# More deferred products per routing hop, gathered rows turned by TensorE, and a new order for the last dense experts

## The chip, the cores and the metric

The kernel runs on one core of a Trainium2 chip. The metric is the device time of one execution in microseconds (us). Three runs of the kernel before gave 862.59, 863.86 and 866.21 us; their median, 863.86 us, is the time that the change is compared with. A separate execution was taken with the profiler.

## The reference

Three layers follow one another on 1536 tokens of 512 numbers. Attention has 8 heads of 64, with a local window of 96 keys and 8 global keys. The first mixture computes all 4 experts for every token and adds them with given shares. The second mixture sends each token to one of 8 experts, 192 tokens to each, in the order of all gate logits:

```python
attn = softmax(q @ k.T * scale + bias) @ v            # per head, masked
x = attn.transpose(0, 2, 1, 3).reshape(1536, 512)
p = domain_probs / (domain_probs.sum(-1, keepdims=True) + 1e-09)
for e in range(4):
    out += p[:, e:e + 1] * (np.maximum(x @ w1[e], 0.0) @ w2[e])
logits = out @ w_gate
for idx in np.argsort(-logits.flatten()):             # 12288 pairs (token, expert)
    tok, e = idx // 8, idx % 8
    if assigned[tok] < 0 and counts[e] < 192:
        assigned[tok] = e; counts[e] += 1
y[mask_e] = np.maximum(out[mask_e] @ v1[e], 0.0) @ v2[e]
```

## The kernel before

Tokens lie in 12 blocks of 128. Numbers are split in two float16 parts, high and low, and a product is made of three matmuls (high by high, high by low, low by high). Weights arrive as float32, 1 MB at a time, and are prepared in steps: ScalarE squares a half (L469, tile `junk`) to find a power of two, TensorE sums over the partitions (L473, tile `pw`), VectorE makes the scale (L330, L334, L335), ScalarE writes the high part (L580, tile `w`) and VectorE the low part (L494, tile `w`). One call of `pump` issues one such step and first starts any load that has a free buffer (`w_load`, L413). Squares of a half are issued only when `wait` pumps have passed since its load was issued (`WAITS`).

The order on each engine is the order in which the program issues; the engines work through it in turn, and so does the DMA queue that SyncE (SP) issues.

**The stage of the last dense experts** (`phase3`, 354 to 571 us of the span) computes the first layers of experts 2 and 3, forms the gate logits of each block and ranks the pairs. Its order is written out by hand in the table `ORDER3`: `a` are products on TensorE, `r`, `h` and `l` the ReLU and its two halves (L862 or L860, L584/L582/L580, L1584; a letter behind a slash gives the engine, A ScalarE, V VectorE, G GpSimd), `mturn` and `turn` transposes of the second-layer weights by DMA (L932, tiles `wth`, `wtl`), `mprod` and `prod` the small products that use them (L940), `start` the end of the preparation of expert 3's weights, `row` a transposed block for the logits (L956), `lm`, `lo`, `rr`, `cm`, `rc`, `ct`, `rk` the logits and the ranking (`ct` on TensorE, L1039; `cm` on VectorE, L1019 to L1024; `rk` writes tile `R`, L1049). `fill` issues a twelfth of a deferred product: the second layers of experts 3 and 2 for one block take 24 matmuls of 512 columns (L1072), two to a fill, 288 fills in all. When a block is done VectorE adds it to `y` (L1086).

**The route** (`route`, 579 to 631 us) finds the cut of each expert in 7 rounds. A round has four hops from VectorE to TensorE and back, and at each hop `between` issues some fills, by the list `HOPS`, and one `pump`. A round counts on TensorE (L1206), reads the count (L1209), spreads it (L1215), and does so twice.

**The tail** (631 to 684 us) issues the remaining fills, three at a time with a pump, and beside them the side work of finished blocks: `add`, a square (L1092), a scale, the two halves of the rows (L1115 to L1120, tile `xs`), and their store to memory (L1123, tensor `rows`).

**The routed experts** (684 us to the end) gather 2 x 96 rows for each expert with an indirect DMA from GpSimd (L1274, tile `g`), turn them so that columns lie on partitions (`gather_T`, a DMA transpose on SP, L1283, tile `xg`) and compute `m_g1` (L1305) and `m_g2` (L1325), with a pump for every step or so. An expert has 96 matmuls of 192 columns in each of its two layers; in the first, every 24 end in one ReLU on ScalarE, `H` (L860).

Of the kernel before, what the change touches and what calls it, by code (L numbers as in the profile page):

```python
# [6 lines left out]
F32 = mybir.dt.float32  # L7
# [125 lines left out]
    mturn3 mprod1 a21 mturn4 xh0/V h0/G pump.7 l0/G pump.8 pump.9 a30 mturn5 a31 xl0 r2/V h1/V a40 row0 l1/G r3/A
    pump.10 pump.11 pump.12 pump.13 h2/G pump.14 mprod2 norm1 a41 pump.15 a50 pump.16 mturn6 a51 pump.17 sc1 mturn7
    l2/G mprod3 xh1/V a60 a61 mgate start h3/A turn0 l3/G turn1 prod0 turn2 r4/A turn3 turn4 a70 a71 xl1 r5/A h4/A
    h5/V turn5 prod1 l4/V row1 prod2 turn6 a00.1 a01.1 r6/V l5/V norm0.1 r7/V h6/G h7/A turn7 sc0.1 sp prod3 l6/G
    r0.1/A l7/G a10.1 gate lm fill a11.1 lo rr xh0.1/G r1.1/V cm1 cm0 rc0 rc1 lm.1 cm2 ct0 ct1 fill.1 rc2 ct2 cm4 cm3
    rc3 rc4 h0.1/G cm5 a20.1 ct3 a21.1 lo.1 cm6 rr.1 ct4 h1.1/V rc5 rc6 cm7 xl0.1 fill.2 ct5 rc7 l0.1/V l1.1/V r2.1/V
    ct6 a30.1 ct7 cm0.1 a31.1 cm1.1 rc0.1 rk a40.1 cm2.1 ct0.1 rc1.1 ct1.1 h2.1/G a41.1 r3.1/A a50.1 rc2.1 cm3.1
    h3.1/A ct2.1 rc3.1 row0.1 ct3.1 cm4.1 l2.1/V a51.1 rc4.1 norm1.1 cm5.1 cm6.1 sc1.1 ct4.1 a60.1 l3.1/V a61.1  # L140
    xh1.1/A a70.1 r4.1/V a71.1 h4.1/A r5.1/V xl1.1 l4.1/V rc5.1 row1.1 a00.2 fill.3 rc6.1 h5.1/G norm0.2 ct5.1 r6.1/V
    l5.1/G a01.2 sp.1 h6.1/G a10.2 r7.1/V fill.4 l6.1/V sc0.2 h7.1/G l7.1/V lm.2 a11.2 xh0.2/A lo.2 ct6.1 rr.2 r0.2/V
    xl0.2 r1.2/A cm0.2 lm.3 fill.5 rc0.2 cm7.1 ct0.2 rc7.1 cm1.2 fill.6 ct7.1 h1.2/G row0.2 cm2.2 fill.7 cm3.2 norm1.2
    a20.2 rk.1 rc1.2 lo.3 rc2.2 ct1.2 ct2.2 fill.8 fill.9 cm5.2 cm4.2 a21.2 rc3.2 sc1.2 rc4.2 ct3.2 h0.2/G rc5.2 a30.2
    l0.2/V cm6.2 ct4.2 r2.2/A ct5.2 l1.2/V rc6.2 fill.10 cm7.2 rr.3 ct6.2 a31.2 cm0.3 cm1.3 r3.2/V rc7.2 rc0.3 ct7.2
    a40.2 h3.2/A xh1.2/V rk.2 h2.2/A rc1.3 xl1.2 cm2.3 ct0.3 row1.2 a41.2 l3.2/G a50.2 rc2.3 a51.2 ct1.3 cm3.3 a60.2
# [15 lines left out]
    h0.5/A ct5.7 cm6.7 l0.5/V a21.5 rc6.7 a30.5 h1.5/V ct6.7 r2.5/A h2.5/A rc7.7 a31.5 rr.8 xl0.5 fill.24 lo.9 l1.5/V
    ct7.7 a40.5 cm0.8 rc0.8 cm1.8 rc1.8 cm2.8 row0.5 rk.7 rc2.8 r3.5/A a41.5 ct0.8 ct1.8 cm4.8 cm3.8 rc4.8 ct2.8 cm5.8
    h3.5/A fill.25 rr.9 a50.5 ct3.8 fill.26 rc5.8 ct4.8 a51.5 ct5.8 cm6.8 a60.5 cm0.9 a61.5 rc6.8 ct6.8 l2.5/G rc0.9
    cm7.8 cm1.9 fill.27 r4.5/A ct7.8 cm2.9 l3.5/G r5.5/A norm1.5 a70.5 rc1.9 rk.8 a71.5 fill.28 fill.29 sc1.5 h4.5/A
# [1716 lines left out]
```

## Time and profile before

| what | value |
|---|---|
| median of three runs | 863.86 us (862.59 to 866.21) |
| the profiled execution's own time | 861.97 us |
| its span | 860.2 us |
| TensorE busy (matmul) | 777.3 us, 90% of the span |
| VectorE busy | 608.4 us, 71% |
| ScalarE busy | 502.2 us, 58% |
| GpSimd busy | 206.4 us, 24% |
| mean granted clock of TensorE | 0.962 of full speed |

Full speed is 2.4 GHz and the other level is 1.2 GHz, 0.5 of it. A busy share is a mean over stages with different limits, so the table only says where to look: TensorE is nearly full, and what it lacks lies in a few stretches. 1.8 us of the execution lie outside the span.

### The profile page before, as it was taken

What the parts mean: (1) busy time and instruction counts of PE and PEld (TensorE: products, weight loads), DVE (VectorE), ACT (ScalarE), POOL (GpSimd) and SP (SyncE); (2) the same over time, 40 slices, a digit from 0 to 9 for tenths busy, and PEclk for the clock granted to TensorE, in tenths of its full rate; (3) what the DMA queues carried; (4) which work ended last, traced back from release to release, by engine and by line L of the source; (5) the groups of instructions that cost most, each with busy time, mean ns of one, the idle gap of its engine ahead of it and who ended that gap; (6) DMA issues with size and microseconds to landing.
All of it is one profiled execution on the core that took longest, in us unless ns stands there. A gap on an engine that the chain in (4) does not pass through costs nothing. (4 is left out here: it accounts for less than half of the span.)

```text
span 860.2 us, 21736 instructions
## 1 busy us (share of the span) xinstructions
PE 777.3 (90%) x8916; PEld 600.1 (70%) x8920; DVE 608.4 (71%) x1467; ACT 502.2 (58%) x1004; POOL 206.4 (24%) x238
## 2 busy tenths in 40 slices
PE   3688999999999999999999999979998757999996
PEld 3477767777777767678888887534443357888996
DVE  5998888777763644547879999986674625797890
ACT  5887786745352323334557979631056417989852
POOL 3553352332442224240210112000000022222221
PEclk9689999999999999999999999989999869999999
DMA  8996769664447311691333320249014279899811
GB/s 272 265 191 140 130 154 171 120 136 88 99 73 207 104 51 51 125 178 31 75 71 69 77 59 26 63 103 330 34 32 140 76 237 332 253 265 335 174 38 38
DMA packets 219652, 116.38 MB, mean 135 GB/s; under 512 B 187424, under 2 KB 187424, under 8 KB 219552
## 3 DMA queue, kind: packets, MB, share of 16 engines
q1 hardware_dynamic: 217504, 108.64, 50.6%
q0 software_dynamic: 2048, 6.34, 3.1%
q8 instruction: 70, 1.15, 0.6%
q14 instruction: 30, 0.25, 0.1%
HBM read 69.30 MB, written 12.63 MB: 95 GB/s over the span
## 5 line engine op out<-in xcount | busy, mean ns | idle before, releaser
L886 PEld LDWEIGHTS <-w 128*128 128x128 f16 x3456 | 248.1, 98 | 37.9 <-issue 4.1
L886 PE MATMUL pH<-xT,w 128*128 128x128 f16 (+1 forms) x3168 | 252.9, 235 | 2.2 <-ACT H L860 1.6
L1072 PE MATMUL pY<-w,xT 128*128 128x512 f16 x384 | 120.7, 386 | 4.6 <-DVE y L1086 4.6
L897 PE MATMUL pY<-w,hh 128*128 128x512 f16 x384 | 114.7, 381 | 0.0
L1033 ACT ACTIVATE Cj<-C 128x256 bf16<-128x256 bf16 (+11 forms) x88 | 75.3, 855 | 28.2 <-DVE C L1024 21.6
L1305 PEld LDWEIGHTS <-w 128*128 128x128 f16 x768 | 66.4, 101 | 28.5 <-DMA xg<-g 16.2
L1072 PE MATMUL pY<-w,hl 128*128 128x512 f16 x192 | 74.1, 386 | 0.0
L897 PE MATMUL pY<-w,hl 128*128 128x512 f16 x192 | 73.1, 381 | 0.0
L860 ACT ACTIVATE H<-pH 128x512 f32<-128x512 f32 (+1 forms) x70 | 38.4, 554 | 55.1 <-PE pH L886 34.4
L1305 PE MATMUL pH<-xg,w 128*128 128x192 f16 x528 | 51.5, 259 | 19.5 <-DMA xg<-g 17.0
L1072 PEld LDWEIGHTS <-xT 128*128 128x128 f16 x384 | 36.5, 99 | 42.1 <-issue 8.6
L1325 PE MATMUL pR<-hh,w 128*128 128x192 f16 x512 | 64.9, 246 | 0.0
L1325 PEld LDWEIGHTS <-w 128*128 128x128 f16 x768 | 63.3, 98 | 2.0 <-issue 1.9
L1325 PE MATMUL pR<-hl,w 128*128 128x192 f16 x256 | 63.0, 246 | 0.0
L1022 DVE TENSOR_SCALAR C<-w,Lg 128x1024 bf16<-128x1024 f32 (+7 forms) x98 | 58.8, 615 | 0.6 <-PE pw L1039 0.4
L762 ACT ACTIVATE t<-pS,mx,ec 128x256 f32<-128x256 f32 (+1 forms) x96 | 51.6, 541 | 2.2
L777 POOL TENSOR_TENSOR pp<-t,pp 128x512 f16<-128x512 f32 (+1 forms) x34 | 40.1, 1183 | 44.4 <-ACT pp L580 35.9
L494 DVE SCALAR_TENSOR_TENSOR w<-w,wsr,w 128x1024 f16<-128x1024 f32 x32 | 40.4, 1279 | 10.0 <-ACT w L580 9.9
L584 DVE TENSOR_SCALAR hh<-H 128x384 f16<-128x384 f32 (+1 forms) x53 | 20.9, 396 | 37.5 <-ACT H L860 37.0
L897 PEld LDWEIGHTS <-hh 128*128 128x128 f16 x384 | 32.9, 98 | 19.6
L1452 POOL TENSOR_TENSOR hl<-H,hh 128x512 f16<-128x512 f32 x26 | 32.9, 1265 | 56.3 <-DVE hh L584 31.7
L469 ACT ACTIVATE junk<-w 128x2048 f16<-128x2048 f32 x16 | 30.5, 1906 | 25.4 <-DMA w<-in_moe_w_dram 25.4
(298 smaller groups left out, 1537.7 us busy)
## 6 DMA issues: line engine op xcount, KB each, us to landing
w<-in_moe_w_dram SPq DMA_DIRECT2D x16, 1024.0 KB, 13.0
raw<-in_moe_w_dram SPq DMA_DIRECT2D x16, 1024.0 KB, 7.8
hl<-in_moe_w_dram SPq DMA_DIRECT2D x8, 1024.0 KB, 5.5
y<-in_moe_w_dram SPq DMA_DIRECT2D x4, 1024.0 KB, 6.7
xT<-in_moe_w_dram SPq DMA_DIRECT2D x4, 1024.0 KB, 11.5
rows<-xs SPq DMA_DIRECT2D x12, 260.0 KB, 2.1
x<-in_k_dram SPq DMA_DIRECT2D x12, 256.0 KB, 3.3
x<-in_q_dram SPq DMA_DIRECT2D x12, 256.0 KB, 3.9
```

The lines of the kernel that those rows point to most:

```text
L494: V.scalar_tensor_tensor(l, r[:, d2], sc, h, op0=OP.mult, op1=OP.subtract)
L762: s.nc.scalar.activation(t[:, hh], ps[:, hh], AF.Exp, bias=mx[:, 1, hh:hh + 1], scale=e[:, 0:1], accum_out=s.SU[j][:, 2 * g + hh:2 * g + h ...
L777: (G if eng == "G" else V).tensor_sub(pl[:, x], t, ph[:, x])
L860: s.nc.scalar.activation(H, ps, AF.Relu, scale=HS)
L886: nc.tensor.matmul(o[f], w[:, d, 128 * (f0 + f):128 * (f0 + f) + 128], x[:, :, c], start=(d == 0 and i == 0), stop=(d == 3 and i == 2))
L897: nc.tensor.matmul(py, l[:, f], w[:, f], start=(f == 0 and i == 0), stop=(f == 7 and i == 2))
L1022: V.tensor_scalar(C[:, 8 * i:8 * i + n], x[:, :n, e], l, None, op0=OP.is_ge)
L1033: s.nc.scalar.activation(x, C, AF.Copy, accum_out=s.AC[j][:, 1, e:e + 1])
L1072: nc.tensor.matmul(py, a[:, f], w[:, f], start=(n == 0), stop=(n == 23))
L1305: nc.tensor.matmul(ps[0][:, f % 2], w[:, d, 128 * f:128 * f + 128], xg[:, :, c], start=(k == 0), stop=(k == 11))
L1325: nc.tensor.matmul(ps[0][:, d % 2], w[:, f, 128 * d:128 * d + 128], h[:, f], start=(k == 0), stop=(k == 23))
L1452: (nc.gpsimd if eng == "G" else nc.vector).tensor_sub(x[1], P.pop((e, j, c)), x[0])
```

## The change

Four things change. The order of `phase3` is another one (the same 775 entries; two lines of the table are shown). The hops of rounds 2 to 7 issue 8, 2, 5 and 1 fills where they issued 8, 1, 4 and 1. In the tail the pumps stop when 18 or fewer fills are left, and none goes with the side work; `WAITS[1]`, the wait before squares in the stage of the routed experts, goes from 13 to 18. And the gathered rows of experts 0 and 1 are turned by 32 matmuls against the identity, which ScalarE and VectorE copy out of PSUM, four copies each; experts 2 to 7 keep the DMA transpose.

```diff
-    norm0 sc0 a00 pump pump.1 mturn0 a01 pump.2 mturn1 a10 pump.3 pump.4 pump.5 pump.6 r0/A mprod0 a11 r1/V a20 mturn2
+    pump a00 mturn0 pump.1 pump.2 pump.3 pump.4 mturn1 norm0 pump.5 a01 a10 mturn2 r0/A mturn3 pump.6 sc0 xh0/A xl0
...
-HOPS = [0, 1, 4, 1, 8, 1, 4, 1, 8, 1, 4, 1, 8, 1, 4, 1, 8, 1, 4, 1, 8, 1, 4, 1, 8, 1, 4, 1, 4, 7]
-WAITS = [4, 13, 6, 2]
+HOPS = [0, 1, 4, 1] + [8, 2, 5, 1] * 6 + [4, 7]
+LASTFILLS, PUMPR = 18, 1
+WAITS = [4, 18, 6, 2]
...
+    def gather_turn(s, e):
+        nc, g = s.nc, s.GX[e]
+        xg = s.ex.tile([128, 2, 8, 96], F16, name="xg")
+        for u in range(2):
+            for a in range(2):
+                ps = s.pH.tile([128, 4, 96], F32, name="pH")
+                for i in range(4):
+                    nc.tensor.matmul(ps[:, i], g[:, u, 512 * a + 128 * i:512 * a + 128 * i + 128], s.identh[:96, :96],
+                                     start=True, stop=True)
+                o = xg[:, u, 4 * a:4 * a + 4]
+                if a:
+                    nc.vector.tensor_copy(o, ps)
+                else:
+                    nc.scalar.activation(o, ps, AF.Copy)
+        s.GX[e], s.GG[e] = xg, g
...
             while fills:
                 fill(3)
-                s.pump(1)
+                if len(fills) > LASTFILLS:
+                    s.pump(PUMPR)
             while s.side:
                 s.side_step()
-                s.pump(1)
...
-            s.gather_T(0)
-            s.gather_T(1)
+            s.gather_turn(0)
+            s.gather_turn(1)
             s.rawfree += [raw2] * 4 + two(s.wc, 1)
             s.loadlimit = len(s.jobs)
             s.pump(WAITS[3])
```

In the table the engines of some entries change too. Over the stage VectorE has 14 `r` where it had 18, 10 `h` where it had 7, and 27 `l` where it had 29; for the first pair of blocks GpSimd has 3 `l` where it had 6. `start` comes after the ten products to `a41`; it came after the fourteen to `a61`.

The order on SP around the gathers, before: stores of rows, the four transposes of gathered rows, then eight loads of weights of 1 MB (`raw`, `w_11172`, `w_10031`).

```order
L413 DMA w_10031<-in_moe_w_dram 128x4x512
L1123 DMA rows<-xs 128x1040 x3
L413 DMA w_10031<-in_moe_w_dram 128x4x512
L1123 DMA rows<-xs 128x1040 x9
L1283 DMA_TRANSPOSE xg<-g 128x8x96 x4
L413 DMA raw<-in_moe_w_dram 128x4x512 x5
L413 DMA w_11172<-in_moe_w_dram 128x4x512 x2
L413 DMA w_10031<-in_moe_w_dram 128x4x512
L1283 DMA_TRANSPOSE xg<-g 128x8x96 x2
```

The same place now (the changed file's lines are one higher here):

```order
L1124 DMA rows<-xs 128x1040 x3
L414 DMA w_10031<-in_moe_w_dram 128x4x512 x2
L1124 DMA rows<-xs 128x1040 x9
L414 DMA raw<-in_moe_w_dram 128x4x512 x5
L414 DMA w_11216<-in_moe_w_dram 128x4x512 x2
L414 DMA w_10031<-in_moe_w_dram 128x4x512
L1284 DMA_TRANSPOSE xg<-g 128x8x96 x2
```

The eight loads no longer stand behind transposes that wait for the gathers, and the first three stores of rows stand ahead of both loads of the tail.

ScalarE at the start of the routed experts, before: high parts of expert 1's first layer, a square, the ReLUs of expert 0 and 1.

```order
L580 ACTIVATE w_11153<-raw,wsr 128x2x512 x2
L580 ACTIVATE w_11153<-w_10031,wsr 128x2x512 x2
L469 ACTIVATE junk,wss<-raw 128x2048
L860 ACTIVATE H<-pH 128x384 x2
L860 ACTIVATE H<-pq 128x384
L580 ACTIVATE w_11287<-w_10031,wsr 128x1024
L860 ACTIVATE H<-pH 128x384
L580 ACTIVATE w_11287<-w_10031,wsr 128x1024
L860 ACTIVATE H<-pH 128x384
L469 ACTIVATE junk,wss<-raw 128x2048 x2
L860 ACTIVATE H<-pq 128x384
```

And now, with the copies of the turned rows (`xg`) in it:

```order
L581 ACTIVATE w_11153<-raw,wsr 128x2x512 x2
L581 ACTIVATE w_11153<-w_10031,wsr 128x2x512
L1301 ACTIVATE xg<-pH 128x384 x4
L581 ACTIVATE w_11153<-w_10031,wsr 128x2x512
L470 ACTIVATE junk,wss<-raw 128x2048
L861 ACTIVATE H<-pH 128x384 x2
L861 ACTIVATE H<-pq 128x384
L581 ACTIVATE w_11331<-w_10031,wsr 128x1024
L861 ACTIVATE H<-pH 128x384
L581 ACTIVATE w_11331<-w_10031,wsr 128x1024
L861 ACTIVATE H<-pH 128x384
L581 ACTIVATE w_11331<-raw,wsr 128x1024
```

The copies stand ahead of one high part and of the first square, and the two squares that stood behind the fifth ReLU come later.

## Rows read from the trace of the kernel before

**Rows 1.** Busy time by stretch: us, PE, PEld, DVE, ACT, POOL (instructions), clock, DMA, GB/s.
```profile
354.40:390.00 35.60, 32.96 (x415) 28.96 (x414) 18.72 (x47) 10.13 (x16) 10.87 (x10) 0.95 0.95 157
480.00:553.00 73.00, 71.98 (x972) 57.80 (x969) 70.28 (x201) 58.84 (x108) 13.16 (x17) 1.00 0.22 56
553.00:571.00 18.00, 13.11 (x144) 6.97 (x143) 17.69 (x50) 12.61 (x17) 0.24 (x3) 0.81 0.36 89
631.00:684.00 53.00, 45.65 (x224) 20.23 (x221) 30.55 (x61) 30.79 (x58) 0.98 (x9) 0.97 0.27 91
698.00:730.00 32.00, 25.86 (x260) 24.89 (x261) 14.23 (x35) 19.05 (x25) 4.86 (x4) 0.87 1.04 328
730.00:800.00 70.00, 64.55 (x769) 62.77 (x767) 56.32 (x96) 67.36 (x86) 18.72 (x22) 1.00 1.02 285
```

**Rows 2.** Timeline at the turned weights of expert 3, ScalarE and TensorE.
```profile
367.62 0.60 ACT L860 ACTIVATE H<-pH 128x512 f32<-128x512 f32 x1 [6.17 <-POOL hl L1584]
...
380.82 0.18 PE L940 MATMUL pq<-wg,wtl 128*128 128x8 f16 x1 [1.92 <-DMA wtl<-w]
```

**Rows 3.** Who TensorE waited for, 320 to 580 us: total, times, longest.
```profile
PE pw L1039 <- DVE R L1049: 4.2, 2, 3.1
PE pq L940 <- DMA wtl<-w: 2.6, 2, 1.9
```

**Rows 4.** VectorE's groups, 354 to 571 us: count, busy us, mean ns, idle before; one `h`.
```profile
L1584 DVE TENSOR_TENSOR hl<-H,hh 128x512 f16<-128x512 f32 x15 | 11.1, 748 | 0.2 <-ACT hh L580 0.2
L862 DVE TENSOR_SCALAR H<-pH 128x512 f32<-128x512 f32 x12 | 8.1, 684 | 2.4 <-PE pH L886 2.3
...
394.69 0.42 DVE L584 TENSOR_SCALAR hh<-H 128x512 f16<-128x512 f32 x1
```

**Rows 5.** One round of the route: busy time, two rows of TensorE, one of VectorE.
```profile
602.91:610.47 7.56, 7.56 (x55) 3.36 (x55) 4.47 (x18) 0.00 (x0) 0.00 (x0) 1.00 0.19 69
...
607.07 0.59 PE L1072 MATMUL pY<-w,xT 128*128 128x512 f16 x2
607.72 0.59 PE L1072 MATMUL pY<-w,xT 128*128 128x512 f16 x2
...
610.47 0.19 DVE L1209 TENSOR_SCALAR_CACHE_REDUCE vt<-pq 8x40 f32<-8x40 f32 x1 [1.19 <-PE pq L1206]
```

**Rows 6.** Timeline of the tail: a square on ScalarE, and the last low part on VectorE.
```profile
657.03 1.91 ACT L469 ACTIVATE junk<-w 128x2048 f16<-128x2048 f32 x1 [2.96 <-DMA w<-in_moe_w_dram]
...
664.83 0.59 PE L1072 MATMUL pY<-w,xT 128*128 128x512 f16 x2 [2.00 <-DVE y L1086]
...
666.66 1.28 DVE L494 SCALAR_TENSOR_TENSOR w<-w,wsr,w 128x1024 f16<-128x1024 f32 x1 [1.45 <-ACT w L580]
```

**Rows 7.** Chain that ended last, from the last rows to the first routed product.
```profile
685.89 2.02 DMA rows<-xs
...
693.19 3.96 DMA g<-rows,idx
```

**Rows 8.** Issues of gathers at 693, 718 and 758 us, and transposes at 693: median us to landing.
```profile
xg<-g SPq DMA_TRANSPOSE x2, 3.5
g<-rows,idx POOLq DMA_INDIRECT x1, 4.0
...
g<-rows,idx POOLq DMA_INDIRECT x1, 6.6
...
g<-rows,idx POOLq DMA_INDIRECT x2, 11.3
```

**Rows 9.** Timeline between the tail and the routed experts: VectorE, TensorE, SP.
```profile
685.77 2.48 DVE L494 SCALAR_TENSOR_TENSOR w<-raw,wsr,w 128x1024 f16<-128x1024 f32 x2
...
697.92 6.63 PE L1305 MATMUL pH<-xg,w 128*128 128x192 f16 x48 [15.71 <-DMA xg<-g]
698.48 4.64 SPq L413 DMA_DIRECT2D raw<-in_moe_w_dram  x5
```

**Rows 10.** ScalarE and TensorE at the start of the routed experts: timeline, then a wait.
```profile
704.05 1.91 ACT L469 ACTIVATE junk<-raw 128x2048 f16<-128x2048 f32 x1 [15.20 <-DMA raw<-in_moe_w_dram]
...
724.78 0.47 ACT L860 ACTIVATE H<-pH 128x384 f32<-128x384 f32 x1
...
PE pw L473 <- ACT junk L469: 6.5, 6, 1.9
```

**Rows 11.** Turning by TensorE earlier in the kernel: ns min/median/max, first and last start.
```profile
L664 PE MATMUL pH<-identh,xs x8: 219/258/315, 46.9 to 48.0; 128*128 128x128 f16 x8
```

More of the change, by code (lines that the diff above doesn't have):

```diff
@@ L131 @@
 ORDER3 = """
-    norm0 sc0 a00 pump pump.1 mturn0 a01 pump.2 mturn1 a10 pump.3 pump.4 pump.5 pump.6 r0/A mprod0 a11 r1/V a20 mturn2
[L133 to L146, printed above, removed]
@@ L162 @@
[L162 to L165, printed above, removed]
-    ct0.9 ct1.9 l4.5/G h5.5/A fill.30 cm4.9 fill.31 rc2.9 fill.32 r6.5/A fill.33 l5.5/V cm3.9 h6.5/A fill.34 r7.5/A
@@ new lines @@
+    pump.7 mprod0 a11 mturn4 a20 h0/V l0/G r1/V pump.8 a21 pump.9 h1/A mprod1 mturn5 a30 pump.10 mturn6 pump.11 l1/G
+    mturn7 row0 pump.12 mprod2 a31 pump.13 r2/V mprod3 norm1 pump.14 a40 h2/V mgate a41 pump.15 pump.16 pump.17 r3/V
+    start l2/V r4/A a50 h3/A a51 turn0 sc1 a60 turn1 turn2 xh1/V prod0 a61 turn3 xl1 l3/G prod1 a70 a71 r5/A turn4
+    turn5 h5/G h4/A prod2 l4/V a00.1 row1 l5/V turn6 turn7 norm0.1 r6/A h6/G prod3 a01.1 r7/A h7/G gate a10.1 l7/V
+    l6/V lm sc0.1 lo a11.1 xh0.1/A r0.1/V rr a20.1 cm0 cm2 cm1 rc0 ct0 rc1 ct1 sp rc2 cm3 ct2 rc3 lm.1 ct3 xl0.1 fill
@@ new lines @@
+    cm6 cm5 fill.1 h0.1/V fill.2 r1.1/A fill.3 cm4 rc4 rc5 h1.1/A ct4 l0.1/G lo.1 rc6 row0.1 a21.1 ct5 ct6 cm7 l1.1/G
+    rc7 rr.1 cm0.1 r2.1/A cm1.1 a30.1 ct7 rc0.1 rc1.1 fill.4 a31.1 rk norm1.1 ct0.1 r3.1/V h2.1/A a40.1 cm2.1 ct1.1
+    rc2.1 a41.1 l2.1/V sc1.1 cm3.1 rc3.1 ct2.1 cm4.1 cm5.1 xh1.1/V rc4.1 rc5.1 h3.1/G xl1.1 a50.1 ct3.1 ct4.1 r4.1/V
+    cm6.1 a51.1 l3.1/V a60.1 r5.1/V a61.1 row1.1 a70.1 a71.1 norm0.2 a00.2 rc6.1 h4.1/A l4.1/V r6.1/A h5.1/G sc0.2
+    ct5.1 l5.1/G ct6.1 a01.2 cm7.1 r7.1/A h7.1/A a10.2 h6.1/G l6.1/V r0.2/A l7.1/G fill.5 xh0.2/A lm.2 lo.2 a11.2
@@ new lines @@
+    xl0.2 r1.2/V rr.2 cm0.2 sp.1 rc0.2 lm.3 fill.6 rc7.1 ct0.2 lo.3 ct7.1 cm1.2 h0.2/A cm3.2 fill.7 a20.2 rc1.2 cm2.2
+    row0.2 a21.2 rc2.2 rk.1 rc3.2 ct1.2 h1.2/A rr.3 ct2.2 ct3.2 cm5.2 l0.2/V fill.8 fill.9 cm4.2 cm6.2 rc4.2 r2.2/A
+    rc5.2 a30.2 ct4.2 rc6.2 ct5.2 l1.2/G ct6.2 h2.2/V cm7.2 a31.2 cm0.3 rc7.2 a40.2 r3.2/A cm1.3 rc0.3 ct7.2 a41.2
+    rk.2 ct0.3 a50.2 rc1.3 h3.2/V ct1.3 cm2.3 a51.2 norm1.2 rc2.3 cm3.3 ct2.3 rc3.3 ct3.3 fill.10 sc1.2 cm5.3 a60.2
+    l2.2/V xh1.2/V l3.2/G cm6.3 cm4.3 rc4.3 a61.2 xl1.2 a70.2 r4.2/A r5.2/V rc5.3 a71.2 h5.2/A row1.2 ct4.3 h4.2/V
@@ new lines @@
+    fill.39 rc5.9 lo.10 cm6.9 rr.10 ct5.9 lm.11 fill.40 fill.41 cm0.10 fill.42 fill.43 rc0.10 lo.11 rc6.9 rr.11 ct0.10
+    ct6.9 cm3.10 fill.44 cm1.10 fill.45 cm7.9 fill.46 fill.47 rc1.10 fill.48 fill.49 fill.50 ct1.10 ct7.9 fill.51
+    fill.52 fill.53 cm2.10 fill.54 rc2.10 ct2.10 fill.55 cm4.10 fill.56 rk.9 fill.57 rc4.10 fill.58 fill.59 ct3.10
+    fill.60 cm5.10 cm6.10 fill.61 fill.62 ct4.10 fill.63 rc5.10 ct5.10 rc6.10 fill.64 fill.65 fill.66 cm0.11 fill.67
+    fill.68 rc0.11 fill.69 fill.70 cm7.10 ct6.10 fill.71 cm1.11 fill.72 ct7.10 ct0.11 fill.73 rc1.11 cm2.11 rk.10
@@ L176 @@
+    ct1.11 rc2.11 cm3.11 ct2.11 cm4.11 cm5.11 ct3.11 cm6.11 rc4.11 rc5.11 fill.74 rc6.11 fill.75 fill.76 fill.77
+    ct4.11 fill.78 fill.79 fill.80 ct5.11 fill.81 fill.82 fill.83 fill.84 sp.5 ct6.11 fill.85 fill.86 fill.87 cm7.11
+    fill.88 ct7.11 fill.89 fill.90 fill.91 fill.92 fill.93 fill.94 rk.11 fill.95
 """.split()
```

44 lines of the change are left out of this document (20 added, 24 removed).

## The prediction

> **What bounds the kernel now.** I read the busy time by stretch first, then who TensorE waited for, then the timelines of the places that the change touches.
>
> In the stage of the last dense experts TensorE works 32.96 of the first 35.6 us, at a mean clock of 0.95, and VectorE only 18.72 [rows 1]. From 480 us on VectorE is full too: 70.28 of 73 us, then 17.69 of 18 while TensorE falls to 13.11 [rows 1]. What ends the stage is VectorE's ranking; TensorE waits 4.2 us for it there [rows 3].
>
> In the route a round takes 7.56 us, and TensorE is busy in all of them [rows 5]. In the tail TensorE idles 53 - 45.65 = 7.35 us with no other engine full [rows 1]. The stalls start on ScalarE: a square waits 2.96 us for its weights, VectorE's low part waits for the high part behind it, and TensorE stands 2.00 us because the sum of a finished block (L1086) comes late and its PSUM buffer with it [rows 6].
>
> Between the last rows and the first routed product everything is idle but the chain: rows to memory, gathers, transposes [rows 7, 9]. From 698 to 730 us TensorE works 25.86 of 32 us, at 0.87 of its clock; from 730 to 800 us ScalarE is full, 67.36 of 70 [rows 1]. So the routed experts run at ScalarE's pace, and how early it gets its work decides.
>
> A difference under 0.5%, 4.3 us, is about what a measurement of this kernel cannot tell from none.
>
> **The order of the last dense experts.** The same work is issued in another order, so nothing is removed on TensorE. What can be won is idle time: 35.6 - 32.96 = 2.64 us at the start, with 5% of clock there, some 1.8 us [rows 1], and 3.0 us of VectorE's own idle time from 480 us on (2.72 + 0.31) [rows 1]. That is 7.4 us, the lower end of the time. VectorE's work gets 4 `r` less at 0.684, 3 `h` more at 0.42 and 2 `l` less at 0.75 us: -2.74 + 1.26 - 1.50 = -3.0 us [rows 4]. The other end: the eight transposes for `mprod` now come in a row and `mprod2` and `mprod3` two products earlier or more; two waits like the longest of before, 1.92 us [rows 2], would cost 4 us where about 2.6 are lost now, so some 2 us worse allowing for the clock.
>
> I take -3 us, for one reason that rows carry. ScalarE stood 6.17 us at 367.6 us behind a GpSimd `l` [rows 2]; the last high parts of expert 3's weights were queued behind that, then their transposes, and at their end TensorE stood 1.92 us [rows 2]. Now GpSimd has half of those `l`, and `start` is issued four products earlier, so these transposes begin about that ReLU's wait, half of it or more, sooner. The 1.92 us and most of the clock's 1.8 go, less what arises anew. The end of the stage keeps its order (the last counts wait for VectorE as before), so I expect no more from there than VectorE's 3.0 us of work would allow, and count none of it. What is late next is row 11's comparisons on VectorE.
>
> **The hops.** Twelve fills move out of the tail into six rounds. A fill is two matmuls; three start in 607.72 - 607.07 = 0.65 us, so 0.43 us a fill [rows 5]. The rounds grow by 2 x 0.43 = 0.86 us each, 5.2 in all, and the tail shrinks by 12 x 0.43 = 5.2. VectorE's wait at a hop (1.19 us) is already a wait for TensorE [rows 5]: that hop is over-covered, and more products cover nothing more there. At a spread, one fill covers slightly less than VectorE needs; about 0.1 us a round is won, 0.5 us in all.
>
> **The tail.** Its ScalarE work, 30.79 of 53 us [rows 1], must now fit beside 5.2 us less of fills. The three early rows move into the route, their two halves of about 0.7 us with them. The pumps that are dropped hold nothing before: the last low part is at 666.66 us [rows 6], and the last 18 fills, 7.8 us, begin at about 674. So that edit costs nothing and wins nothing, covered by pumps having run dry; should they not have, weight steps move behind the last row, 1.13 to 1.28 us each. The squares that stall the tail keep their four pumps of distance. I take 0 for the tail, with ends of -4 (half its idle time goes) and +3 (a shorter tail with the same ScalarE work stalls more). Hops and tail together: -0.5.
>
> **Gathers, turning, weights.** Three effects.
>
> First, the loads. The first of them now waits only until its buffer is free, after the low parts that end at 685.77 + 2.48 = 688.25 us; it was issued at 698.48 [rows 9]. Ten us sooner, seven MB are in flight while the four gathers go out. That is new: a gather alone landed 4.0 us after its issue, with the loads running 6.6, and once 11.3 [rows 8]. I take 6.6, since the row at 718 us has the same eight loads outstanding; the last gather lands at 693.19 + 6.6 = 699.8 us where it was 697.15 [rows 7].
>
> Second, the turning. Before, expert 0's products began at 697.92, as the last gather landed [rows 9]; expert 1's transposes ran beside them. Now both experts are turned first. Of the 32 matmuls only the last 8 come after the last gather: 0.15 us apart at most (eight within 1.1 us [rows 11]), with a copy of about 0.5, some 1.5 us. The first product comes at 701.3 us, 3.4 late.
>
> The Trainium skill, Advanced Engine Details and Errata, X-Bar Transpose (TRN2), says that transposing DMAs run as fast as ordinary ones, which speaks against TensorE here. The rows agree without load: 3.5 us for a transpose against 4.0 for a gather [rows 8]. By that rule the turning would only cost its 1.5 us; the sum above does not use it.
>
> Third, ScalarE. Its first square waited 15.20 us for a load and started at 704.05 [rows 10]. Now the four copies stand ahead of it, until about 701, then a high part; the square ends at 704.4, two us earlier than before, and no later one waits for a load. TensorE's sums wait for squares: 6.5 us in all [rows 10]. With `WAITS[1]` at 18 they are issued 36 matmuls later, and TensorE, 3.4 us late, reaches the first of them without stopping. Following the new order, with 2.0 us for a square, 1.04 for a high part and 0.4 for a ReLU, the eighth ReLU ends at 722.1 us where it ended at 725.15 [rows 10], with one square (2.0) still to do that was done before and one high part (1.04) done that was not. ScalarE is 2.0 us ahead, and from there it sets the pace to 800 us. I take -2. Ends: -5 if gathers land as fast as alone, +3 if they take 11.3 us.
>
> **The sum**: 861.97 - 3.0 - 0.5 - 2.0 = 856.5 us against the profiled execution's own time. The median of the three runs stands 1.9 us above it, so 858.4 us for the median.
>
> **Rivals.**
>
> *The last stage wins nothing.* VectorE's ranking ends that stage at 97% busy [rows 1], and time won 100 us earlier is lost waiting for it. Against: VectorE is half idle in the first part and has 3.0 us less to do. It gives 863.9 - 2.5 = 861.4 us.
>
> *Gathers land as if alone.* The queues of GpSimd and SP would share fairly, so 200 KB need not wait for megabytes. For: a gather is a fifth of a load. Against: 6.6 us and more in every loaded row [rows 8]. The product starts 2.6 us sooner: 855.8 us. The Trainium skill, DMA: Bandwidth & Descriptors, Queues, rings and completion order, says that each DMA engine goes round its queues a packet at a time; by that rule this rival would hold, and so far the loaded rows speak against it.
>
> *Gathers wait behind the weights.* This is the way to a slower kernel. If the seven MB drain first, at the 380 GB/s or so of that stretch (the mean from 698 to 730 us is 328 [rows 1]), they take 18 to 21 us from 688.3, and the gathers land at 707 to 710. ScalarE and VectorE stand behind their copies until then, and the clock falls again. 7.2 to 10 us more than I took make the third term +5 to +8, and the time 865.6 to 868.6 us. It decides when the last gather lands after 705 us, where the third term eats the others. For: the 11.3 us row. Against: the row at 718 us.
>
> *The hops cost, the tail does not pay.* If ScalarE's 30.8 us of work set the tail's length, the rounds still grow 5.2 us: 863.6 us.
>
> **How the numbers follow.** Forecast 0.45, nothing from the last stage 0.22, gathers as if alone 0.16, gathers behind weights 0.10, hops that cost 0.07. Faster by over 0.5% means under 859.5: two thirds of the forecast's cases (0.31), all of the second rival's 0.16, and a little of the first's; 0.50. Slower means over 868.2: half of the third rival, and a few hundredths from each case whose bounds add up badly; 0.13. The rest, 0.37, is no difference. The range runs from 850 (the forecast with the lower ends of two terms) to 867 us (the third rival's middle).
>
> **What would show it.** The sums for expert 3's gate at 381 us without a wait of 1.9 us, and the clock full there. Rounds of 8.3 to 8.4 us. Loads of `raw` issued by 689 us relative to the same last row; gathers of 6 to 7 us; the first routed product some 15 us after the last row's store begins where it was 12. No wait for squares between the sixth and the eighth ReLU. I am wrong if the last dense stage ends later than before, if ScalarE is not ahead at the eighth ReLU, or if the gain lies in the tail, where I see none.

## The result, and the profile after

The changed kernel takes 855.16 us (median, 853.41 to 858.65) where the kernel before, run beside it, takes 864.9 (862.59 to 866.21): a ratio of 0.9896, 95% interval 0.9863 to 0.9929, or 9.7 us less by the medians. 858.4 had been forecast, within 850 to 867. Run again among the experiments it gave 0.9911 (0.9890 to 0.9933). The medians of before lay between 862.0 and 865.2 us from one set of runs to another, so what follows compares ratios.

The profiled execution is the slowest of its four, 858.65 us with a span of 856.9. What lies ahead of the last dense experts, which the change does not touch, ends 1.8 us later in it than in the profile of before. Line numbers are higher than before by one, and by 18 behind the gathers. Busy time by stretch, after, at the places of [rows 1] (us, PE, PEld, DVE, ACT, POOL, granted clock, DMA share, GB/s; the DMA share is the time that packets took, as a share of the 16 engines' span):

```profile
356.20:391.80 35.60, 33.81 (x453) 30.24 (x452) 20.97 (x54) 13.36 (x25) 6.33 (x6) 1.00 0.95 157
482.00:555.00 73.00, 72.19 (x921) 57.11 (x919) 68.57 (x197) 59.19 (x108) 11.99 (x17) 0.98 0.22 49
636.00:678.00 42.00, 40.95 (x215) 18.66 (x211) 29.11 (x63) 29.60 (x52) 0.98 (x9) 1.00 0.31 111
697.30:729.30 32.00, 28.27 (x304) 27.14 (x303) 18.24 (x39) 25.19 (x31) 5.32 (x4) 0.91 0.81 267
```

In the first 35.6 us of the last dense experts TensorE idles 1.8 us where it was 2.6, at full clock where it was 0.95. In the tail it idles 1.05 us of 42, where it was 7.35 of 53. In the first 32 us of the routed experts ScalarE works 25.2 us where it was 19.1.

The turned weights of expert 3, on TensorE's timeline, then who TensorE waited for from 320 to 582 us:

```profile
382.53 0.18 PE L941 MATMUL pq<-wg,wth 128*128 128x16 f16 x1 [0.16 <-DMA wth<-w]
383.65 0.18 PE L941 MATMUL pq<-wg,wtl 128*128 128x8 f16 x1 [0.94 <-DMA wtl<-w]
```

```profile
PE pw L1040 <- DVE R L1050: 2.3, 1, 2.3
PE pw L1040 <- DVE C L1020: 1.7, 2, 1.5
PE pq L941 <- DMA wtl<-w: 1.6, 2, 0.9
```

The wait of 1.92 us in [rows 2] is now 0.94, and the sum over both turned weights 1.6 where it was 2.6 [rows 3]. The ranking still ends the stage.

One round of the route, after; [rows 5] had 7.56 us:

```profile
602.45:610.86 8.41, 8.41 (x59) 3.74 (x59) 5.14 (x18) 0.00 (x0) 0.00 (x0) 1.00 0.46 142
```

The gathers and the first routed products: the median landing of the four gathers, SP's loads, the first product, who waited for squares until 745 us.

```profile
g<-rows,idx POOLq DMA_INDIRECT x4, 7.3
```

```profile
683.91 6.36 SPq L414 DMA_DIRECT2D raw<-in_moe_w_dram  x5
...
697.26 2.97 PE L1323 MATMUL pH<-xg,w 128*128 128x192 f16 x19 [0.26 <-ACT xg L1301]
...
717.28 0.47 ACT L861 ACTIVATE H<-pH 128x384 f32<-128x384 f32 x1
```

```profile
PE pw L474 <- ACT junk L470: 0.7, 2, 0.5
```

The first gather is issued at 684.55 us (688.83 before, GpSimd's timeline). Against it the first product comes at 12.7 us (9.1 before) and the eighth ReLU ends at 33.2 (36.4 before): 3.2 us ahead. But then, at expert 4:

```profile
767.07 3.04 PE L1323 MATMUL pH<-xg,w 128*128 128x192 f16 x24 [2.99 <-DMA xg<-g]
770.70 1.91 ACT L470 ACTIVATE junk<-w 128x2048 f16<-128x2048 f32 x1 [5.06 <-DMA w<-in_moe_w_dram]
```

The same square in the profile of before:

```profile
774.06 1.91 ACT L469 ACTIVATE junk<-w 128x2048 f16<-128x2048 f32 x1 [2.64 <-DMA w<-in_moe_w_dram]
```

The ten us ahead of the wait in the kernel after, and the ten behind:

```profile
754.55:764.55 10.00, 9.53 (x116) 9.29 (x113) 9.86 (x18) 9.98 (x16) 2.52 (x5) 1.00 1.13 160
764.55:774.55 10.00, 7.48 (x72) 7.24 (x73) 3.56 (x7) 4.94 (x7) 1.95 (x3) 0.83 1.03 344
```

ScalarE, full until then, waits 5.06 us for a load that was issued at 757.34 us and took 13.3 us to land: in the ten us ahead of the wait the DMA engines are busy at a share of 1.13 and move only 160 GB/s. Before waited 2.64 us at this square, so 2.4 us are lost there. By the last row of TensorE all of the 3.2 us, and 0.9 more, are gone in this profile; where the rest went was not followed.

Stage by stage, from the first and last rows of each in the timelines, us. The last dense stage runs from the last product of the stage before it to the last write of `R`; route and tail from the first count to the last fill, so that a moved fill does not show; the last three columns are counted from the issue of the first gather.

| kernel | last dense | route + tail | first product | 8th ReLU | last TensorE row |
|---|---|---|---|---|---|
| before | 222.3 | 102.5 | 9.1 | 36.4 | 163.8 |
| after | 222.9 | 95.8 | 12.7 | 33.2 | 164.7 |
| after, second profile | 220.1 | 95.8 | 12.5 | 32.9 | 162.5 |
| order alone | 220.2 | 100.7 | 9.0 | 36.3 | 162.7 |
| hops alone | 224.2 | 95.8 | 9.1 | 36.1 | 166.7 |
| 6 fills | 223.7 | 99.8 | 9.3 | 36.7 | 166.8 |
| 24 fills | 223.8 | 96.2 | 9.2 | 36.2 | 166.9 |
| gathers alone | 224.3 | 100.5 | 13.0 | 34.4 | 161.9 |
| turning, 13 pumps | 224.0 | 100.7 | 12.8 | 38.1 | 168.1 |
| 18 pumps alone | 224.1 | 101.1 | 9.1 | 32.0 | 156.9 |
| all but the turning | 221.2 | 95.7 | 9.3 | 32.5 | 161.6 |

A stage whose order is the same differs by up to 2.8 us from one execution to another (last dense: 222.3 to 224.3 with the old order, 220.1 to 222.9 with the new, and those two are the same kernel), so a single profile settles no term of 1 or 2 us there; the ratios do. Part of it is TensorE's clock: in the profile of after the granted clock falls to half, 1.2 GHz, for some 3 us around 540 us while TensorE is busy. Over the 5 us below it is 0.66 of full speed, which costs 0.34 x 5 = 1.7 us.

```profile
538.00:543.00 5.00, 5.00 (x66) 3.69 (x64) 4.25 (x16) 1.96 (x3) 0.00 (x0) 0.66 0.18 67
```

Of the seven profiles with the new order only this one and that of the run with expert 4 turned too show the fall, 222.9 and 223.0 us; the other five took 220.1 to 221.2, on average 220.7. TensorE works 4.59 of the 5 us ahead of the fall, and just as much at this place of the second profile of the same kernel, where the clock stays full; why it falls in some executions is open.

### The profile page after: what moved, and what is told of

The parts are those of the page before. It is cut to its first block, busy times and chain, and to the rows that moved or that the text cites. A ratio compares the mean times of both kernels' runs of the same rounds, so it can differ in the third digit from the quotient of the medians.

```text
span 856.9 us, 21798 instructions
## 1 busy us (share of the span) xinstructions
PE 780.5 (91%) x8952; PEld 603.5 (70%) x8952; DVE 612.5 (71%) x1468; ACT 506.9 (59%) x1014; POOL 205.0 (24%) x235
## 5 line engine op out<-in xcount | busy, mean ns | idle before, releaser
L1343 PE MATMUL pR<-hh,w 128*128 128x192 f16 x512 | 67.1, 249 | 0.0
L861 ACT ACTIVATE H<-pH 128x512 f32<-128x512 f32 (+1 forms) x69 | 38.1, 553 | 44.0 <-PE pH L887 28.7
L1073 PEld LDWEIGHTS <-xT 128*128 128x128 f16 x384 | 36.3, 99 | 36.7 <-issue 2.2
L1323 PE MATMUL pH<-xg,w 128*128 128x192 f16 x528 | 49.2, 252 | 4.7 <-DMA xg<-g 3.0
L495 DVE SCALAR_TENSOR_TENSOR w<-raw,wsr,w 128x1024 f16<-128x1024 f32 x32 | 40.3, 1279 | 12.8 <-ACT w L581 12.6
L898 PEld LDWEIGHTS <-hh 128*128 128x128 f16 x384 | 32.9, 98 | 19.5
L1470 POOL TENSOR_TENSOR hl<-H,hh 128x512 f16<-128x512 f32 x26 | 32.9, 1264 | 56.8 <-DVE hh L585 31.8
## 6 DMA issues: line engine op xcount, KB each, us to landing
w<-in_moe_w_dram SPq DMA_DIRECT2D x16, 1024.0 KB, 12.7
```

Source lines behind the costliest of these rows:

```text
L495: V.scalar_tensor_tensor(l, r[:, d2], sc, h, op0=OP.mult, op1=OP.subtract)
L861: s.nc.scalar.activation(H, ps, AF.Relu, scale=HS)
L898: nc.tensor.matmul(py, l[:, f], w[:, f], start=(f == 0 and i == 0), stop=(f == 7 and i == 2))
L1073: nc.tensor.matmul(py, a[:, f], w[:, f], start=(n == 0), stop=(n == 23))
L1323: nc.tensor.matmul(ps[0][:, f % 2], w[:, d, 128 * f:128 * f + 128], xg[:, :, c], start=(k == 0), stop=(k == 11))
L1343: nc.tensor.matmul(ps[0][:, d % 2], w[:, f, 128 * d:128 * d + 128], h[:, f], start=(k == 0), stop=(k == 23))
```

## The experiments

**One part at a time.** The order of the last dense experts alone:

```diff
 kernel before
-    norm0 sc0 a00 pump pump.1 mturn0 a01 pump.2 mturn1 a10 pump.3 pump.4 pump.5 pump.6 r0/A mprod0 a11 r1/V a20 mturn2
+    pump a00 mturn0 pump.1 pump.2 pump.3 pump.4 mturn1 norm0 pump.5 a01 a10 mturn2 r0/A mturn3 pump.6 sc0 xh0/A xl0
...
```

> The kernel before with the new order of the last dense experts and nothing else. The prediction took 3.0 us from it: 861.9 us against a median of 864.9, and from the stage's first product to the last write of R about 219.5 us where the trace of before shows 222.5. The rival (VectorE's ranking ends the stage, the time won early is lost waiting for it): no change, 864.9 +- 1, the stage 222 to 223 us. The changed kernel's trace speaks for the rival: 223.1 us, and TensorE waits 2.3 + 1.5 us for the ranking at its end. If the rival holds, the two stalls for turned weights are shorter and the idle time in front of the last counts is longer than before.

Measured: 0.9979 (0.9962 to 0.9996), 1.8 us less. The stage takes 220.2 us. With all profiles of the table the new order has a mean of 221.1 us in four and the old one 223.8 in seven. TensorE's waits for the turned weights are shorter in each of the new ones, 1.4 to 1.6 us where the old ones have 2.6 to 3.0, and so is its wait for the ranking, 2.3 us where it was 4.2 to 4.8. The prediction's 3.0 lies inside the interval (0.3 to 3.3 us); the rival that nothing is won lies just outside it.

The hops alone:

```diff
 kernel before
-HOPS = [0, 1, 4, 1, 8, 1, 4, 1, 8, 1, 4, 1, 8, 1, 4, 1, 8, 1, 4, 1, 8, 1, 4, 1, 8, 1, 4, 1, 4, 7]
+HOPS = [0, 1, 4, 1] + [8, 2, 5, 1] * 6 + [4, 7]
```

> The kernel before with the new list of hops alone (the pumps that the changed tail leaves out issue nothing, so this is hops and tail together). The prediction took 0.5 us: 864.4 us, rounds of 8.4 us, the tail 5.2 us shorter and its two stalls of 2.0 us still there. The theory from the two traces: the stalls of the tail go with the new hops, because the three early rows and a block's sum no longer stand between a weight's high and low part on VectorE; the tail, from the last round's last count to the last fill, shrinks by about 11.9 us while the route grows by 5.2: 858.2 us. A third reading, that the gain is only there with the gathers' part behind it: the first gather comes 6 to 7 us earlier and the total still falls by under 2 us.

Measured: 0.9937 (0.9915 to 0.9960), 5.4 us less; route and tail together 95.8 us where before has 102.5, and the other kernels with the old hops 100.5 to 101.1. The pump edit is no part of this: in the route and the tail the profiles with and without it (hops alone, all but the turning) have the instructions in the same order on every engine. So the largest gain of the three parts lies where none had been forecast.

The gathers' part alone (turning, loads ahead, 18 pumps):

```diff
 kernel before
-WAITS = [4, 13, 6, 2]
+WAITS = [4, 18, 6, 2]
...
-            s.gather_T(0)
-            s.gather_T(1)
+            s.gather_turn(0)
+            s.gather_turn(1)
```

> The kernel before with the turning by TensorE, the loads ahead of it and squares after 18 pumps, and nothing else. The prediction took 2.0 us: 862.9 us, the last gather landing 6.6 us after its issue, the eighth ReLU 3 us earlier against the first gather's issue. By the changed kernel's trace the eighth ReLU comes 3.2 us earlier against the first gather's issue, but 2.4 us of it are lost again at a load for a square of expert 4 (ScalarE waits 5.1 us there where it waited 2.6), so no more than 1 us is left: 864 to 865 us. If the gathers fell behind the loads: the last lands after 9 us and the time is over 867 us.

Measured: 0.9983 (0.9967 to 0.9999), 1.5 us less. The product came 3.9 us later and the eighth ReLU 2.0 earlier; the wait for a load came at another place than expected, 2.95 us for `raw` 103 us after the first gather.

The whole change once more, unedited:

> The changed kernel once more, for its profile and for the sum of the three parts under the same runs of before. 855.2 us as measured, 9.7 below before. If the parts add up, the three gains above sum to that. The wait of ScalarE for the load of expert 4's weights comes again at 4 to 6 us if it is of the order of the transfers, and not if it was one execution's chance.

Measured: 0.9911 (0.9890 to 0.9933). The three parts sum to 1.01% and the whole gives 0.89%, the same within the intervals. ScalarE's wait for expert 4's load came again, 3.97 us.

**Why the tail got shorter: how many fills.**

```diff
 hops alone
-HOPS = [0, 1, 4, 1] + [8, 2, 5, 1] * 6 + [4, 7]
+HOPS = [0, 1, 4, 1] + [8, 2, 5, 1] * 3 + [8, 1, 4, 1] * 3 + [4, 7]
```

> The kernel before with 6 more fills in the rounds, not 12: only the first three of the six lengthened rounds. Theory (the tail's stalls come from the work of the three early rows and of a finished block, which stands on VectorE and ScalarE at the tail's start; it must be done in the route): half a block is not enough to take the three early rows out of the tail, so the route grows by 2.6 us, the tail shrinks by 2.6 and one or two of the stalls of 2 us stay; 0 to 3 us below before. Rival (each fill moved out of the tail gains by itself): half of what 12 gained, 2.7 us below before, with the stalls halved and none gone.

Measured: 0.9982 (0.9956 to 1.0007), and TensorE's timeline in the tail still shows the waits for a block's sum:

```profile
649.26 0.59 PE L1073 MATMUL pY<-w,xT 128*128 128x512 f16 x2 [1.17 <-DVE y L1087]
660.34 0.59 PE L1073 MATMUL pY<-w,xT 128*128 128x512 f16 x2 [0.56 <-DVE y L1087]
667.59 0.59 PE L1073 MATMUL pY<-w,xT 128*128 128x512 f16 x2 [1.86 <-DVE y L1087]
```

```diff
 hops alone
-HOPS = [0, 1, 4, 1] + [8, 2, 5, 1] * 6 + [4, 7]
+HOPS = [0, 1, 4, 1] + [8, 3, 6, 1] * 6 + [4, 7]
```

> The kernel before with 24 more fills in the rounds (8, 3, 6 and 1). Theory: nothing is left to gain, since with 12 the tail had no stall left; route 59 us, tail 36.7 us, the time as with 12, 5 us below before. Rival one (each fill gains by itself): 10 us below before. Rival two (the loads of the tail and ScalarE's squares then set its length, 30.8 us of work with three loads in series between): the tail stays above 38 us with stalls on VectorE's sums, and 1 to 3 us of the gain are lost again.

Measured: 0.9951 (0.9920 to 0.9982); route and tail 96.2 us, and the first gather 7.6 us after the last fill where it was 6.6. 24 fills win nothing more than 12, so that each moved fill gains by itself falls (24 would have given 0.9874, outside the interval). Between 6 and 12 the ratios alone do not tell a step from a slope, for half of what 12 gave, 0.9969, lies inside the interval of 6. In the profiles it is a step: with 6 fills the stalls are still there, with 12 and with 24 the tail has none.

What the step is shows when before and hops alone are laid side by side. Before, from all engines: the index product that ends the route, the first half of the three early rows, weight steps, a load of weights and the stores of the three rows, then the square, the low part and the sum that follow that load, and TensorE waiting for the sum.

```profile
635.38 0.70 PE L1264 MATMUL pq<-gt,Coh 128*96 128x16 f16 x12 [1.00 <-DVE Coh L1259]
635.84 0.72 ACT L580 ACTIVATE xs<-y,rgr 128x512 f16<-128x512 f32 x1 [1.67 <-DVE rgr L335]
...
638.46 1.13 ACT L580 ACTIVATE w<-w,wsr 128x1024 f16<-128x1024 f32 x1
639.62 1.28 DVE L494 SCALAR_TENSOR_TENSOR w<-w,wsr,w 128x1024 f16<-128x1024 f32 x1 [1.97 <-ACT w L580]
...
640.91 2.06 DVE L1120 SCALAR_TENSOR_TENSOR xs<-y,rgr,xs 128x512 f16<-128x512 f32 x3
640.93 0.38 SPq L413 DMA_DIRECT2D w<-in_moe_w_dram  x1
641.71 1.78 SPq L1123 DMA_DIRECT2D rows<-xs  x3
...
647.19 1.91 ACT L469 ACTIVATE junk<-w 128x2048 f16<-128x2048 f32 x1 [1.54 <-DMA w<-in_moe_w_dram]
...
650.26 1.28 DVE L494 SCALAR_TENSOR_TENSOR w<-w,wsr,w 128x1024 f16<-128x1024 f32 x1 [4.93 <-ACT w L580]
651.46 0.75 DVE L1086 SCALAR_TENSOR_TENSOR y<-pY,pe,y 128x512 f32<-128x512 f32 x1
...
652.26 0.59 PE L1072 MATMUL pY<-w,xT 128*128 128x512 f16 x2 [2.04 <-DVE y L1086]
```

Hops alone: the stores of the three rows, the last low half of them, the index product, and the same chain. No row of TensorE with a wait follows until the tail's end.

```profile
636.04 6.75 SPq L1124 DMA_DIRECT2D rows<-xs  x3
...
641.58 0.75 DVE L1121 SCALAR_TENSOR_TENSOR xs<-y,rgr,xs 128x512 f16<-128x512 f32 x1
...
641.72 0.70 PE L1265 MATMUL pq<-gt,Coh 128*96 128x16 f16 x12 [1.00 <-DVE Coh L1260]
...
642.56 1.13 ACT L581 ACTIVATE w<-w,wsr 128x1024 f16<-128x1024 f32 x1
642.91 2.47 DVE L495 SCALAR_TENSOR_TENSOR w<-w,wsr,w 128x1024 f16<-128x1024 f32 x2
...
645.41 9.77 SPq L414 DMA_DIRECT2D w<-in_moe_w_dram  x2
...
650.40 1.91 ACT L470 ACTIVATE junk<-w 128x2048 f16<-128x2048 f32 x1 [2.26 <-DMA w<-in_moe_w_dram]
...
653.48 1.28 DVE L495 SCALAR_TENSOR_TENSOR w<-w,wsr,w 128x1024 f16<-128x1024 f32 x1 [4.73 <-ACT w L581]
654.68 0.74 DVE L1087 SCALAR_TENSOR_TENSOR y<-pY,pe,y 128x512 f32<-128x512 f32 x1
```

The low part ahead of the sum comes 14.9 us after the index product before and 11.8 with the new hops, 3.1 us sooner against the fills, and TensorE, which stood 2.04 us behind the sum, no longer waits. In both it waits for a high part, whose square waits for the load. So follow the load. Before, it goes out as the low part of 639.62 ends, 5.6 us after the index product. That low part waits 1.97 us for its high part on ScalarE, and ahead of this high part ScalarE waits 1.67 us for the scale of the early rows and writes the first half of them. With the new hops these halves are written during the route, where both engines have idle time [rows 5], and the load goes out 3.7 us after the index product: 1.9 us sooner. It also takes 5.0 us where it took 6.3 with the stores of the early rows right behind it: another 1.3. The next load follows, 13.1 us after the index product where it was 16.2. VectorE's 2.06 us for the low halves of the early rows are not in this chain, for it waits 4.93 us behind them.

This is no chance of one profile: the load goes out 5.6 us after the index product in all five profiles with the old hops and 3.7 in all seven with 12 fills moved, and 6.1 us with 6 fills, which is why they leave the stalls, and 3.0 with 24. That the early rows are what holds the load back rests on these rows and on the step between 6 and 12; moving the rows without the fills was not tried.

**Why the gathers' part gives so little: turning against waiting.**

```diff
 gathers alone
-WAITS = [4, 18, 6, 2]
+WAITS = [4, 13, 6, 2]
```

> The gathers' part alone as before, but the squares of the routed experts after 13 pumps as in the kernel before, so that only the turning and the earlier loads are changed. If the later squares carry the gain, TensorE waits for squares again between the fourth and the eighth ReLU, 3 us or more, the eighth ReLU ends 36 to 37 us after the first gather's issue (before: 36.4, with 18 pumps 34.4), and the time is that of before or 1 to 2 us more. If the early loads carry it, 34 to 35 us and the time of gathers alone, 0.2% below before.

Measured: 1.0003 (0.9979 to 1.0027); TensorE waits for squares again (four times until 745 us, 4.9 us) and the eighth ReLU ends at 38.1. The turning and the early loads win nothing by themselves.

```diff
 kernel before
-WAITS = [4, 13, 6, 2]
+WAITS = [4, 18, 6, 2]
```

> The kernel before with squares of the routed experts after 18 pumps where it was 13, and nothing else: transposes by DMA, loads behind them. The turning with early loads but 13 pumps gave nothing (1.0003), with 18 pumps 0.2%. If the later squares carry the gain by themselves, TensorE waits for no square before the eighth ReLU, which ends 33 to 35 us after the first gather's issue (before: 36.4), and the time is 2 us or more below before. If they need the early loads (ScalarE's first square waits 15 us for a load, and squares put off later only crowd the next expert): 36 us or more and no change of the time, 0 to 1 us either way.

Measured: 0.9898 (0.9856 to 0.9940) on four executions of it, and who TensorE waited for from 696 to 745 us:

```profile
PE pH L1323 <- DMA xg<-g: 15.7, 1, 15.7
PE pw L474 <- ACT junk L470: 2.5, 3, 1.4
```

One number in a list gives by itself more than the whole of the gathers' part: 6.1 us of waits for squares in that stretch before become 2.5, the eighth ReLU ends at 32.0 us, and no load is late at expert 4. The intervals of this kernel and of gathers alone (0.9967 to 0.9999) do not overlap: with the old order and the old hops, turning with the loads ahead gave most of it back.

```diff
 whole change
-            s.gather_turn(0)
-            s.gather_turn(1)
+            s.gather_T(0)
+            s.gather_T(1)
```

> The whole change without its turning: order, hops and the wait of 18 pumps as changed, the rows of experts 0 and 1 turned by transposing DMAs with the loads behind them, as in the kernel before. Theory (the later squares carry the gathers' part alone, 1.0% below before by themselves, and turning on TensorE with the loads ahead gives most of that back: 0.2% with both): the product comes 9.1 us after the first gather's issue, the eighth ReLU at 32.0 instead of 32.9 to 33.2, the end at 157 instead of 162.5 to 164.7, and the time is 5 to 8 us below the whole change, 1.5 to 1.8% below before. Rival one (the turning is worth its cost once hops and order are there, because the routed experts then run against the transfers anyway): within 2 us of the whole change, 0.9 to 1.1% below before, with ScalarE's wait of 4 to 5 us for a load of expert 4 still there. Rival two (the four fast runs of the wait alone were chance): 0.7 to 0.9% below before, the end at 163 us.

Measured: 0.9867 (0.9842 to 0.9893), 853.06 us beside 864.38 of before, 11.3 us less and the fastest kernel by ratio here. Against the whole change (0.9896 and 0.9911) that is 0.3 to 0.4%, some 3 us, less than the 5 to 8 expected, and the intervals overlap: it points to a cost of the turning, and does not prove it in this surrounding. Two waits for loads stand on ScalarE, where the whole change had 5.06 and 2.38 us at these squares and the waits alone had none:

```profile
766.51 1.91 ACT L470 ACTIVATE junk<-w 128x2048 f16<-128x2048 f32 x1 [2.52 <-DMA w<-in_moe_w_dram]
803.59 1.91 ACT L470 ACTIVATE junk<-w 128x2048 f16<-128x2048 f32 x1 [2.54 <-DMA w<-in_moe_w_dram]
```

**Is TensorE needed for the turning once the loads go ahead?**

```diff
 whole change
-            s.gather_turn(0)
-            s.gather_turn(1)
             s.rawfree += [raw2] * 4 + two(s.wc, 1)
             s.loadlimit = len(s.jobs)
             s.pump(WAITS[3])
+            s.gather_T(0)
+            s.gather_T(1)
```

> The whole change, but the rows of experts 0 and 1 turned by the transposing DMAs as before, issued behind the eight loads. By the trace of before a transpose takes 3.5 us without load, 8 us and more with loads running: the last gather lands some 11.6 us after the first one's issue, the first product comes at 17 to 20 us where turning by TensorE gives 12.5, and the time is 4 to 7 us above that of the whole change, some 858 to 861. The rule that a transposing DMA is as fast as an ordinary one gives no loss to load: product at 15 us, 2.5 us above the whole change. The third way: the transposes of expert 0 do not wait for the gathers of expert 1, and with two gathers in at 9 us the product starts at 12 to 13 us, no slower than TensorE.

Measured: 1.0047 (1.0018 to 1.0077), some 12 us above the whole change, the first product 28.3 us after the first gather. None of the three cases in the expectation had it so late. SP's queue and TensorE:

```profile
688.88 7.94 SPq L414 DMA_DIRECT2D w<-in_moe_w_dram  x3
696.93 14.78 SPq L1284 DMA_TRANSPOSE xg<-g  x4
```

```profile
711.71 5.98 PE L1323 MATMUL pH<-xg,w 128*128 128x192 f16 x48 [34.91 <-DMA xg<-g]
```

```diff
 the kernel just above
-            s.gather_T(0)
-            s.gather_T(1)
+            s.gather_T(0, nc.scalar)
+            s.gather_T(1, nc.scalar)
```

> The same as the run before it (loads ahead, rows of experts 0 and 1 turned by transposing DMAs), but the four transposes are issued by ScalarE, whose queue holds no loads. In the run before, the first transpose went out at 705.5 us, 10 us after the last gather had landed, and landed 2.8 to 6.1 us after that. Theory (it stood behind the loads in SP's queue; the transfer itself is no slower than 6 us): now the transposes go out as the gathers land and land 4 to 6 us later, expert 0's first product 15 to 18 us after the first gather's issue (28.3 in the run before, 12.5 with TensorE), and the time is 2 to 5 us above the whole change. Rival (the load on the transfer engines itself slows them): product after 22 us and more, whatever the queue.

Measured: 0.9976 (0.9943 to 1.0009), some 6 us above the whole change; the first product at 21.0 us, between the two expectations. The queues of SP (q1) and ScalarE (q10) from 682 to 712 us with packets, MB and share, the issues with their median time to landing, and ScalarE's first square:

```profile
q1 hardware_dynamic: 4224, 8.39, 81.0%
q10 hardware_dynamic: 3200, 0.79, 12.9%
...
g<-rows,idx POOLq DMA_INDIRECT x4, 8.3
xg<-g ACTq DMA_TRANSPOSE x4, 10.4
...
702.20 1.91 ACT L470 ACTIVATE junk<-raw 128x2048 f16<-128x2048 f32 x1 [20.58 <-issue]
```

Of the 15.8 us between 28.3 and TensorE's 12.5, 7.3 go when the transposes leave the queue of the loads: their issue begins 8.1 us after the first gather where it was 13.5 behind the loads. The rest stays, for a transpose that took 3.5 us without load [rows 8] took 10.4 here; that is a single value, as only one of the four has a landing in the trace. The run does not part the effects cleanly. Issuing the four takes ScalarE 12.3 us, so its first square starts at 702.20 us, and three of the eight loads go out from 700.27 on only, after a transpose has landed.

**The wait at expert 4.**

```diff
 whole change
-                    s.gather_T(e + 2)
+                    (s.gather_turn if e == 2 else s.gather_T)(e + 2)
```

> The whole change, and the rows of expert 4 turned by TensorE as well: 32 matmuls more on TensorE (3.3 us) and eight copies, two DMA transposes fewer where the DMA engines' busy share is over 1.1 and they move 150 to 190 GB/s only. In the whole change TensorE waits 1.8 to 3.0 us for those transposes and ScalarE 4 to 5 us for a load of expert 4. If the transposes are what takes the DMA's time there, both waits fall to under 1 us, and the gain of 2 to 4 us, less 1 to 2 for the work added on the full ScalarE, is 1 to 2 us: 0.2% below the whole change. If the loads themselves are the limit, ScalarE's wait stays at 3 us or more and the time is that of the whole change or 1 to 3 us above.

Measured: 0.9939 (0.9913 to 0.9965), by the ratios some 3 us slower than the whole change, though the intervals overlap. ScalarE's wait at expert 4 is gone, as expected if the transposes take the transfers' time; it is no proof, for what is held up ahead of it gives the load more time. The copies stand behind squares in ScalarE's order, and TensorE waits for them ahead of expert 3's first product:

```profile
750.59 0.33 PE L1295 MATMUL pH<-identh,g 96*128 96x96 f16 x4 [3.54 <-ACT xg L1301]
```

## Why the prediction was right, and where not

It forecast 858.4 us, 5.5 less than the median of before, and 9.7 or 7.7 less were measured (the second from 0.9911 of 862.0). The sign and the range held, the size fell short by 2 to 4 us. By its own steps:

- **The last dense experts, -3.0:** -1.8 by ratio, -2.7 by the means of the profiles, and -3.1 without those in which the clock fell. The place was right: half of the 1.92 us and the clock at the start came back. The end gave something too, which the prediction counted as none: VectorE's ranking still sets it, but TensorE waits 2.3 us for it where it was 4.2 [rows 3].
- **The hops and the tail, -0.5:** this step failed. The rounds grew as worked out, to 8.41 us, 5.2 in all; the 0.1 us a round that was to come back at a spread is not seen in this. The tail is where it went wrong. The prediction said that the squares that stall the tail keep their four pumps of distance, and took 0 for the tail, with -4 as its end; 5.4 us were measured. It had listed the halves of the three early rows as moving into the route, and costed them as work that moves along with its fills. But they also hold back a load: at the tail's start they stand ahead of the high part that frees its buffer, and their stores run beside it. That delays the chain of load, square, high part and low part by 3.1 us, and a sum that TensorE needs stands at the end of that chain. The text had named the gain's place as what would prove it wrong; that is where it was.
- **The pumps, 0:** right, the order of route and tail is the same without them.
- **Gathers, turning and weights, -2.0:** -1.5 measured. Gathers at 7.3 us for the 6.6 taken, the product 3.6 us late for 3.4, the eighth ReLU 3.2 us sooner for the 3.05 worked out (with a square to do later and a high part done sooner, 2.2 us ahead for 2.0). That this term came out near is luck all the same, for its credit is wrong: the prediction let `WAITS[1]` only remove an obstacle, and built the 2 us on copies, loads and a first square that comes sooner. Alone, the waits give 1.0% and the rest takes most of it back with the old order and hops; in the whole change it costs 0.3 to 0.4%, not clear of noise. That ScalarE's lead would not last to 800 us, where it meets loads that land late, was not priced either; DMA shares of 1.02 stood in [rows 1].
- **The rivals.** That the last stage wins nothing fell. Gathers neither landed as if alone (4.0) nor behind the weights: 7.3 us, though the first five loads take 12.9. The Trainium skill, DMA: Bandwidth & Descriptors, Queues, rings and completion order, says that each DMA engine goes round its queues; that the gathers land before loads that were issued ahead of them agrees with it. Beside the loads they took 3.3 us longer. The hops paid in the tail.
- **The rule on transposing DMAs.** The Trainium skill, Advanced Engine Details and Errata, X-Bar Transpose (TRN2), would have them as fast as ordinary ones. By the time to landing the traces mostly agree: without load 3.5 us against 4.0 for a gather of the same rows [rows 8], and beside loads, some 30 us after the first gather, 6.0 to 7.9 us for transposes where gathers took 6.4 to 8.3, over six kernels (7.9 against 6.4 in before, 6.0 against 7.7 in all but the turning). Only the 10.4 us above speaks against it. What they take of the engines is another matter: 12.9% of 30 us for 0.79 MB, where 8.39 MB of loads took 81.0%, an estimate of 204 GB/s of engine time against 345.
- **One chance.** The prediction counted half of the case in which gathers wait behind the weights, 865.6 to 868.6 us, as slower than 868.2; nearly all of that span lies below it, so its chance of a slower kernel was too high by its own numbers.

Open: why the waits for loads at expert 4 come and go. With the stage in its old order they were 2.6 to 5.5 us in five profiles, with turning and 18 pumps none, 4.0 and 5.1 in three, and a profile each does not tell chance from cause. Whether the parts add up is open too: order, hops and 18 pumps sum to 1.86%, together they gave 1.33%, and the intervals allow that.

## What to carry to other kernels

Work that moves along with a moved piece must be priced at the place it leaves, too: ask which queue it stood in there and who was waiting behind it. When a change bundles a small number with a large rebuild, price the number alone first; here it was worth more than the rebuild. Being ahead on the bounding engine is only a gain as far as the next resource that is full.
